# A window-attention and phase-mixing kernel: one transposition of batch 1 moved from a DMA to TensorE, inside a rewritten list of steps

## The chip, the cores and the metric

The kernel runs on one core of a Trainium2 chip. The metric is the device time of one launch in microseconds (us). The kernel before takes 169.82 us, the median of three runs (169.81, 169.82 and 170.51).

## What is computed

The reference is an attention layer followed by a mixing layer, for 4 batches (B), 8 heads (H), 768 tokens (S) and 64 numbers per head (D).

```python
scores = scale * np.matmul(q, k.transpose(0, 1, 3, 2)) + bias
keep = is_global | is_local            # 8 global keys, and the last 96 positions
a = softmax(np.where(keep, scores, -1e9))
x = np.matmul(a, v)  -> (B, S, H*D) = (4, 768, 512)
theta = x @ w_theta
zr, zi = x * np.cos(theta), x * np.sin(theta)
y = einsum('ts,bsd->btd', w_tok_r, zr) + einsum('ts,bsd->btd', w_tok_i, zi)
u = x + y
out = u + np.maximum(u @ w_ch, 0.0)
```

The bias is a slope of each head times the distance of key and query. The kernel computes in bf16 with sums in f32.

## The kernel before, in words

**Tiles.** Tokens are cut into six tiles of 128, heads are taken in four pairs (so a pair is 128 columns), and the 512 model columns are four chunks of 128, one for each pair. A query tile sees its own key tile, the tile before it and the 8 global keys; therefore the keys of a "tile before" are kept in a second copy (kG, values vG) whose first 8 rows are overwritten with the global ones.

**Steps.** Every piece of work is a small function (lines 198 to 565) that issues its instructions at once. A step is named by its function and its arguments: `m.1.2.0` is function `m_`, batch 1, token tile 2, part 0. For one batch the steps are:

- `lq`, `lv`: loads of q, k and v, issued by GpSimd (POOL) with a cast to bf16. Batch 3's q and k come in another layout (line 86). `lw`, `lt`, `lc` load the weights.
- `pc` (line 306, VectorE): regroups q or k of a pair so that `q` (line 294, TensorE, six 128x128 transpositions) can turn it; `qe` (line 299, VectorE or ScalarE by its letter v or a) copies the result from PSUM to qT or kT. For batch 3 `pd` (line 312) does all of this as one DMA transpose issued by SyncE (SP).
- `kg` (lines 322, 323): the copy kG.
- `s` (line 362, TensorE): scores of two token tiles; `e` (line 374, ScalarE): the exponential; `x` (lines 383, 386, VectorE): times a table of the bias; `v` (line 421, TensorE): times the values; `n` (lines 432, 434, VectorE): division by the sums, which gives a pair of x in x_sb.
- x has to be turned for the product with w_theta. Either `xd` (line 443) turns a pair as one DMA transpose, issued by SP, or `xt` (line 451, six 128x128 transpositions on TensorE into PSUM) and `xe` (line 456, the copy to xT on VectorE or ScalarE) do.
- `th` (line 477, TensorE): theta of two token tiles. Parts 0, 2 and 6 need pairs 0 to 2 of xT, part 3 needs pair 3. `sn` (lines 487, 489, ScalarE): cosine and sine; `z` (line 498, VectorE): times x.
- `m` (line 511, TensorE): a third of the 24 products of one output tile, four matmuls of 512 columns; `u` (line 519, VectorE): plus x. u is turned by `ud` (line 529, a DMA transpose from SP) or by `ut` (line 535) and `ue` (line 539). `c` (line 550, TensorE): times w_ch; `r` (line 558, VectorE): the final sum; `st` (line 564): the store, from SP, or from ScalarE's queue if its part is 1.

Steps that belong to no batch: `warm` (matmuls on zeros), `dist`, `diag`, `swap`, `bt` (tables of the bias), `sb` (the bias of batch 0's scores, laid into PSUM on TensorE), `w`/`we` (weights turned), `cast`, `mv` (ones beside v), `sin` (an activation on one column, which brings the sine table in), `gt` (a copy by which POOL waits for `z`).

**Order.** The whole order is written out by hand: `order` (line 572) is a list of 660 words, each a step, and every engine and queue works through its own part of the list in that order; nothing overtakes on an engine. Semaphores only hold an instruction until its inputs are there and its buffer is free. A step that waits therefore holds back what stands behind it on the same engine, and that goes for SP's queue of DMA transposes and stores too. The digits after the list (line 638) say which of the eight PSUM banks each step that writes PSUM takes.

**Buffers that matter here.** PSUM has eight banks for everything; xT has one buffer; the output tile `o` has four, so a fifth `r` waits for the store of the first; qkn (the regrouped pair) has two, uT five, e three.

In batch 1 the pairs 0 and 1 of x go by `xd`, the pairs 2 and 3 by `xt` and `xe`. In batch 2 the pairs 0 to 2 go by `xd`, pair 3 by `xt`; in batch 3 all go by `xd`.

Of the kernel before, what the change touches and what calls it, by code (L numbers as in the profile page):

```python
# [16 lines left out]
def kernel(  # L17
# [105 lines left out]
    dist = const.tile([T, 6, T], BF)  # L123
# [20 lines left out]
    diag = const.tile([T, H, T], BF)  # L144
# [422 lines left out]
    def do(op, *a):  # L567
        ops[op](*a)
# [1 line left out]


    order = """
        warm.1.3 diag.2 warm.6.0 dist diag.0 bt.6 diag.1 sb.0.1 cast.1.1.a cast.0.0.v warm.3.1 bt.0
        cast.0.1.a diag.3 cast.1.0.v bt.4 q.0.1.0 q.0.0.0 qe.0.1.0.v.2 q.0.0.1 qe.0.0.0.a.0
        qe.0.0.1.a.0 qe.0.0.0.a.1 q.0.1.1 kg.0.0.0.1.v qe.0.0.1.v.1 lw.0 sb.0.0 qe.0.1.1.a.2 swap
        s.0.0.0 kg.0.0.1.4.a sb.0.2 kg.0.1.0.4.v q.0.2.0 lt.0.2 e.0.0.0 q.0.2.1 qe.0.2.0.v.2 lt.2.4
        s.0.0.1 s.0.0.2 e.0.0.1 sb.1.0 qe.0.2.1.v.2 s.0.1.0 warm.1.2 e.0.1.0 sb.1.1 kg.0.2.0.4.v
        sb.1.2 vg.0.0.4 e.0.0.2 s.0.1.1 lw.2 s.0.1.2 sb.2.0 e.0.1.2 v.0.0.0.0.6 v.0.0.1.0.6 e.0.1.1
        s.0.2.0 n.0.0.1.0.6 lq.1.0.8 q.0.3.0 e.0.2.0 q.0.3.1 n.0.0.0.0.6 sb.2.1 qe.0.3.1.a.2
        qe.0.3.0.v.2 s.0.2.1 v.0.1.0.0.6 e.0.2.1 xt.0.0.0.6 sb.3.1 xe.0.0.0.6.v sb.3.0 kg.0.3.0.4.v  # L580
        sb.2.2 mv.1 s.0.2.2 s.0.3.1 n.0.1.0.0.6 e.0.2.2 s.0.3.0 v.0.1.1.0.6 vg.0.4.4 e.0.3.0 sb.3.2
        n.0.1.1.0.6 v.0.2.1.0.6 e.0.3.1 lw.4 v.0.3.2.0.2 n.0.2.1.0.6 s.0.3.2 v.0.2.0.0.6 e.0.3.2
        w.1.0 n.0.3.2.0.2 v.0.3.2.2.4 we.1.0.a w.0.0 n.0.3.2.2.4 xt.0.1.0.6 xt.0.3.0.2 n.0.2.0.0.6
        w.1.1 xe.0.1.0.6.a v.0.3.2.4.6 w.0.1 n.0.3.2.4.6 xe.0.3.0.2.a lc xt.0.2.0.6 bt.1 xt.0.3.2.4
        xt.0.3.4.6 xe.0.3.2.4.v bt.2 xe.0.2.0.6.v th.0.0.4 lv.1.0.8 we.0.1.v we.0.0.v th.0.0.5
        th.0.0.3 th.0.1.2 sn.0.0.0 lq.2.0.8 sn.0.0.1 w.2.0 z.0.0.0 th.0.1.3 xe.0.3.4.6.v w.2.1
        sn.0.1.0 z.0.0.1 th.0.2.2 mv.2 sn.0.1.1 we.1.1.v m.0.1.0 we.2.0.v sin.0 z.0.1.1 th.0.2.3
        m.0.0.0 z.0.1.0 sn.0.2.0 pc.1.1.0 w.3.1 lv.2.0.8 w.3.0 sn.0.2.1 z.0.2.0 q.1.1.0 m.0.0.1
        z.0.2.1 m.0.1.1 we.2.1.v m.0.0.2 pc.1.0.0 bt.3 we.3.1.v bt.7 m.0.1.2 pc.1.0.1 qe.1.1.0.a.2
        pc.1.1.1 we.3.0.v q.1.0.1 q.1.0.0 u.0.0 qe.1.0.1.a.2 q.1.1.1 m.0.2.0 pc.1.3.0 qe.1.0.0.a.2  # L590
        u.0.1 w.4.0 pc.1.2.0 ut.0.0 kg.1.0.0.4.v we.4.0.a m.0.2.2 qe.1.1.1.v.2 ue.0.0.a s.1.0.1
        pc.1.2.1 s.1.0.0 s.1.0.2 kg.1.1.0.4.v e.1.0.0 m.0.2.1 pc.1.3.1 lq.3.0.4 e.1.0.2 q.1.3.1
        m.0.3.0 qe.1.3.1.v.2 e.1.0.1 q.1.2.1 x.1.0.0 ut.0.1 c.0.0.2 ue.0.1.a qe.1.2.1.v.2 q.1.3.0
        x.1.0.2 c.0.1.2 qe.1.3.0.a.2 r.0.0.2 q.1.2.0 bt.5 x.1.0.1 s.1.1.1 qe.1.2.0.a.2 s.1.1.0 u.0.2
        m.0.3.2 r.0.1.2 e.1.1.0 m.0.3.1 kg.1.2.0.4.v e.1.1.1 x.1.1.0 w.4.1 u.0.3 s.1.2.0 s.1.1.2
        s.1.2.1 we.4.1.v e.1.1.2 m.0.4.0 vg.1.0.8 e.1.2.0 ut.0.2 m.0.4.1 ue.0.2.a x.1.1.1
        v.1.0.2.0.6 e.1.2.1 x.1.1.2 w.5.0 n.1.0.2.0.6 kg.1.3.0.4.a w.5.1 ut.0.3 v.1.1.2.0.6 we.5.0.a
        x.1.2.1 xd.1.0 s.1.3.0 ue.0.3.a n.1.1.2.0.6 m.0.4.2 we.5.1.a st.0.1.2 m.0.5.0 e.1.3.0
        x.1.2.0 xd.1.1 pc.2.0.0 s.1.2.2 u.0.4 s.1.3.1 e.1.2.2 s.1.3.2 st.0.0.2 m.0.5.2 pc.2.0.1
        e.1.3.2 x.1.2.2 q.2.0.0 pc.2.1.0 e.1.3.1 c.0.3.2 x.1.3.2 x.1.3.0 qe.2.0.0.a.2 v.1.2.2.0.6  # L600
        x.1.3.1 q.2.0.1 n.1.2.2.0.6 c.0.2.2 v.1.3.2.0.6 pc.2.3.0 pc.2.1.1 xt.1.2.0.6 n.1.3.2.0.6
        q.2.1.0 m.0.5.1 qe.2.1.0.a.2 xe.1.2.0.6.v q.2.1.1 qe.2.0.1.a.2 r.0.3.2 xt.1.3.0.6 th.1.0.0
        u.0.5 kg.2.0.0.4.a th.1.1.0 r.0.2.2 xe.1.3.0.6.a th.1.0.6 qe.2.1.1.v.2 ut.0.4 th.1.0.3
        pc.2.2.0 mv.3 th.1.1.6 kg.2.1.0.4.v sn.1.0.0 th.1.2.0 pc.2.2.1 ue.0.4.v sn.1.0.1 th.1.1.3
        z.1.0.0 ut.0.5 q.2.2.1 sn.1.1.0 th.1.2.6 z.1.0.1 m.1.0.0 vg.2.0.8 pd.3.1.0 sin.1 sn.1.1.1
        th.1.2.3 m.1.1.0 z.1.1.0 st.0.2.2 sn.1.2.0 z.1.1.1 c.0.4.2 gt.1.2 sn.1.2.1 z.1.2.0 lq.3.4.4
        m.1.1.1 r.0.4.2 qe.2.2.1.a.2 m.1.0.1 z.1.2.1 ue.0.5.v s.2.0.2 s.2.0.0 s.2.0.1 m.1.0.2
        e.2.0.0 m.1.1.2 e.2.0.1 u.1.0 c.0.5.2 ud.1.0 e.2.0.2 u.1.1 s.2.1.1 r.0.5.2 s.2.1.0 ud.1.1
        s.2.1.2 e.2.1.0 x.2.0.1 m.1.2.0 lv.3.0.8 pc.2.3.1 pd.3.0.0 x.2.0.0 e.2.1.1 m.1.3.0 x.2.0.2
        q.2.2.0 x.2.1.1 pd.3.2.1 q.2.3.1 qe.2.2.0.a.2 m.1.2.1 qe.2.3.1.v.2 kg.2.2.0.4.a q.2.3.0  # L610
        m.1.2.2 e.2.1.2 qe.2.3.0.v.2 s.2.2.0 u.1.2 s.2.2.2 s.2.2.1 e.2.2.0 x.2.1.2 m.1.3.2 ud.1.2
        e.2.2.1 x.2.2.0 v.2.0.2.0.6 pd.3.1.1 kg.2.3.0.4.v m.1.5.0 e.2.2.2 n.2.0.2.0.6 m.1.3.1
        st.0.3.2 x.2.1.0 xd.2.0 s.2.3.2 x.2.2.1 s.2.3.0 s.2.3.1 e.2.3.0 m.1.5.1 kg.3.2.0.4.v
        st.0.5.2 u.1.3 e.2.3.2 m.1.5.2 x.2.2.2 e.2.3.1 x.2.3.2 c.1.1.2 x.2.3.0 kg.3.1.0.4.a
        v.2.2.2.0.6 x.2.3.1 v.2.1.2.0.6 n.2.2.2.0.6 m.1.4.0 n.2.1.2.0.6 xd.2.2 v.2.3.2.0.6 c.1.0.2
        n.2.3.2.0.6 xd.2.1 m.1.4.1 r.1.1.2 m.1.4.2 pd.3.0.1 r.1.0.2 xt.2.3.0.6 u.1.4 th.2.0.0
        st.0.4.2 xe.2.3.0.6.a u.1.5 pd.3.3.1 th.2.1.0 kg.3.0.0.4.a th.2.0.6 st.1.0.2 th.2.1.6 ud.1.4
        kg.3.3.0.4.v th.2.0.3 th.2.2.0 sn.2.0.0 ud.1.5 th.2.1.3 th.2.2.6 sn.2.0.1 ud.1.3 c.1.2.2
        sin.2 sn.2.1.0 z.2.0.1 c.1.5.2 pd.3.2.0 z.2.0.0 sin.3 sn.2.1.1 th.2.2.3 r.1.2.2 m.2.0.0
        st.1.1.2 z.2.1.0 sn.2.2.0 pd.3.3.0 z.2.1.1 m.2.1.0 r.1.5.2 sn.2.2.1 c.1.3.2 z.2.2.0 m.2.0.1  # L620
        r.1.3.2 z.2.2.1 s.3.0.0 s.3.1.0 e.3.0.0 vg.3.0.8 s.3.0.2 m.2.1.2 e.3.1.0 m.2.1.1 x.3.0.0
        e.3.0.2 m.2.0.2 u.2.1 s.3.2.0 u.2.0 s.3.0.1 e.3.2.0 s.3.2.1 x.3.1.0 m.2.2.0 ud.2.0 e.3.2.1
        c.1.4.2 e.3.0.1 m.2.2.2 r.1.4.2 x.3.0.1 s.3.1.2 s.3.3.0 e.3.1.2 s.3.1.1 x.3.2.1 m.2.3.0
        x.3.0.2 e.3.1.1 x.3.2.0 v.3.0.2.0.6 x.3.1.1 m.2.2.1 e.3.3.0 n.3.0.2.0.6 m.2.3.2 u.2.2 xd.3.0
        s.3.2.2 s.3.3.2 s.3.3.1 e.3.2.2 m.2.3.1 e.3.3.2 ud.2.2 x.3.2.2 m.2.4.0 x.3.1.2 e.3.3.1
        x.3.3.2 st.1.2.2 v.3.1.2.0.6 x.3.3.0 st.1.5.2 v.3.2.2.0.6 u.2.3 m.2.4.2 x.3.3.1 n.3.2.2.0.6
        v.3.3.2.0.6 c.2.0.2 n.3.1.2.0.6 xd.3.2 m.2.5.0 n.3.3.2.0.6 xd.3.1 c.2.2.2 m.2.4.1 ud.2.1
        m.2.5.1 u.2.4 xd.3.3 th.3.0.0 th.3.1.0 st.1.4.2 th.3.0.6 ud.2.3 m.2.5.2 ud.2.4 th.3.0.3
        u.2.5 th.3.1.6 sn.3.0.0 th.3.2.0 st.1.3.2 sn.3.0.1 th.3.1.3 z.3.0.0 th.3.2.6 sn.3.1.0
# [20 lines left out]
_INS = ['q', 'k', 'v', 'n_global', 'n_local', 'moe_w_theta', 'moe_w_tok_r', 'moe_w_tok_i', 'moe_w_ch']  # L650
_OUTS = [((4, 768, 512), 'float32')]
# [30 lines left out]
```

## Time and profile before

| what | us |
|---|---|
| median of three runs | 169.82 |
| the profiled execution's own time | 170.19 |
| its span, from its first to its last instruction | 168.1 |
| TensorE (PE) busy | 154.2 |
| VectorE (DVE) busy | 124.8 |
| ScalarE (ACT) busy | 106.6 |
| GpSimd (POOL) busy | 38.5 |

The profile is one execution. "Busy" of PE overstates its work: matmuls are pipelined, and a matmul's row is longer than the distance to the next one. Idle time in a row is given in brackets with what ended it. DMA rows of SP and POOL show only the issuing; when a transfer lands is told by "to landing" and by the DMA pieces in the chain of waits. Times in the views are us from the start of the span.

### The profile page before, as it was taken

The page shows a single profiled execution, that of the slowest core. Times are in us where ns is not written, and L with a number is a line of the kernel's source. Part 1 is how long each engine was busy: PE and PEld are TensorE (multiplying, and loading weights), DVE is VectorE, ACT ScalarE, POOL GpSimd, SP SyncE. Part 2 cuts the span into 40 slices and gives each one's busy share as a digit, 9 for nine tenths or more (in the row PEclk, how much of TensorE's full clock was granted, in tenths as well). Part 3 has the DMA queues.
Part 4 walks back from the last instruction along what each step waited for, and adds up shares of the span by engine and source line. Part 5 has one row for each costly group of instructions (what it writes and reads, how often), then busy time and mean ns, then how long its engine had stood idle before and what let it go on. Part 6 is the DMA issues. An engine that isn't in the chain of part 4 may idle for free.

```text
span 168.1 us, 3796 instructions
## 1 busy us (share of the span) xinstructions
PE 154.2 (92%) x1547; PEld 86.2 (51%) x1569; DVE 124.8 (74%) x257; ACT 106.6 (63%) x142; POOL 38.5 (23%) x46
## 2 busy tenths in 40 slices
PE   7899999999999996999987798899999999999990
PEld 2456685555657573545553543345557444444450
DVE  7697986978999998695994991588789438543571
ACT  3899899898789937898866115988871349100010
POOL 8975348050352102079400000000000000000000
PEclk9999999999999999999999999999999999999999
DMA  5999999999999999989999998560125674344456
GB/s 150 199 171 177 209 209 203 204 208 188 149 199 193 148 191 149 78 137 121 154 118 146 205 108 207 113 156 4 31 47 158 127 172 174 100 44 125 125 206 231
DMA packets 72704, 25.34 MB, mean 151 GB/s; under 512 B 60784, under 2 KB 69744, under 8 KB 72688
## 3 DMA queue, kind: packets, MB, share of 16 engines
q0 software_dynamic: 45696, 12.45, 82.0%
q1 hardware_dynamic: 26576, 12.13, 34.8%
q10 hardware_dynamic: 416, 0.52, 0.9%
q8 instruction: 12, 0.20, 0.5%
q14 instruction: 4, 0.03, 0.1%
HBM read 25.69 MB, written 6.29 MB: 190 GB/s over the span
## 4 chain that ended last, share of the span: by engine, by line
PE 59%; DMA 18%; DVE 15%; issue 2%; SPq 2%; ACT 1%; POOL 0%; DVEq 0%; POOLq 0%
PE bank L511 27%; PE bank L477 9%; PE bank L550 9%; DMA kT<-qk 8%; DMA xT<-x_sb 6%; PE bank L362 4%; PE bank L421 4%; DMA qk<-in_q_dram 3%; DVE e L383 2%; DVE x_sb L434 2%; DVE kT L299 2%; PE bank L265 2%; SPq L312 1%; DMA uT<-u 1%; DVE kG L322 1%
## 5 line engine op out<-in xcount | busy, mean ns | idle before, releaser
L511 PE MATMUL bank<-zri,w_tokT 128*128 128x512 bf16 x273 | 66.8, 379 | 1.4 <-issue 1.0
L374 ACT ACTIVATE e<-bank 128x1024 bf16<-128x1024 f32 (+1 forms) x48 | 42.9, 955 | 8.9 <-PE bank L362 8.3
L511 PEld LDWEIGHTS <-w_tokT 128*128 128x128 bf16 x288 | 26.5, 98 | 29.5 <-DVE w_tokT L269 0.2
L550 PE MATMUL bank<-w_ch_bf,uT 128*128 128x512 bf16 (+1 forms) x98 | 24.1, 370 | 2.4 <-DVE u L519 1.6
L477 PE MATMUL bank<-w_theta_bf,xT 128*128 128x512 bf16 x92 | 22.8, 379 | 2.9 <-DMA xT<-x_sb 2.7
L519 DVE TENSOR_TENSOR u<-x_sb,bank 128x512 bf16<-128x512 bf16 x24 | 16.2, 684 | 11.2 <-PE bank L511 11.0
L558 DVE SCALAR_TENSOR_TENSOR o<-bank,u 128x512 f32<-128x512 f32 (+1 forms) x25 | 16.2, 666 | 7.9 <-PE bank L550 7.5
L498 DVE TENSOR_TENSOR zri<-x_sb,cs 128x1024 bf16<-128x1024 bf16 (+1 forms) x30 | 16.6, 580 | 6.1 <-ACT cs L489 4.0
L434 DVE TENSOR_TENSOR x_sb<-bank,rec 128x768 bf16<-128x768 f32 (+2 forms) x21 | 16.1, 767 | 0.7
L550 PEld LDWEIGHTS <-uT 128*128 128x128 bf16 x100 | 9.3, 98 | 12.3 <-issue 1.8
L477 PEld LDWEIGHTS <-xT 128*128 128x128 bf16 x96 | 8.8, 97 | 13.0 <-DMA xT<-x_sb 3.9
L539 ACT COPY uT<-bank 128x512 bf16<-128x512 bf16 x5 | 2.9, 589 | 19.1 <-PE bank L535 19.1
L383 DVE TENSOR_TENSOR e<-e,etab 128x1024 bf16<-128x1024 bf16 (+1 forms) x24 | 14.1, 618 | 0.9 <-ACT e L374 0.9
L421 PEld LDWEIGHTS <-e 128*128 128x128 bf16 x352 | 12.6, 97 | 3.3 <-issue 1.0
L362 PE MATMUL bank<-qT,kT 64*128 64x128 bf16 x224 | 12.9, 218 | 0.4 <-DVE qT L299 0.3
L421 PE MATMUL bank<-vn,e 128*128 128x65 bf16 x224 | 13.2, 193 | 0.1
L489 ACT ACTIVATE cs<-bank,halfpi 128x1024 bf16<-128x1024 f32 x8 | 8.9, 1116 | 6.2 <-PE bank L477 6.2
L362 PEld LDWEIGHTS <-kT 64*128 64x128 bf16 x224 | 8.6, 94 | 6.3 <-issue 5.4
L92 POOL DMA_DIRECT2D vn<-in_v_dram x5 | 9.6, 1922 | 8.1 <-DVE qkn L306 6.9
L362 PE MATMUL bank<-qT,kG 64*128 64x128 bf16 x128 | 10.7, 216 | 0.0
L421 PE MATMUL bank<-vG,e 128*128 128x65 bf16 x128 | 10.4, 193 | 0.1
L86 POOL DMA_DIRECT2D qk<-in_q_dram x8 | 6.9, 864 | 12.4 <-issue 4.7
(76 smaller groups left out, 199.1 us busy)
## 6 DMA issues: line engine op xcount, KB each, us to landing
out_dram<-o SPq DMA_DIRECT2D x23, 256.0 KB, 2.4
vn<-in_v_dram POOLq DMA_DIRECT2D x3, 768.0 KB, 23.1
qk<-in_q_dram POOLq DMA_DIRECT2D x2, 768.0 KB, 20.3
qk<-in_k_dram POOLq DMA_DIRECT2D x2, 768.0 KB, 22.3
w_nat<-in_moe_w_tok_r_dram POOLq DMA_DIRECT2D x3, 384.0 KB, 12.3
w_nat<-in_moe_w_tok_i_dram POOLq DMA_DIRECT2D x3, 384.0 KB, 13.5
vn<-in_v_dram POOLq DMA_DIRECT2D x2, 384.0 KB, 9.8
qk<-in_q_dram POOLq DMA_DIRECT2D x8, 96.0 KB, 9.5
```

The source lines that it names most:

```text
L92: nc.gpsimd.dma_start(out=vn[:, h0:h0 + n, :, 0:D].rearrange("p h t d -> p (h t) d"), in_=v[b, h0:h0 + n].rearrange("h (t p) d -> p (h t) ...
L362: nc.tensor.matmul(pb[:, hh, o:o + T], lhsT=lhsT, rhs=qT[R, (own, nxt)[part]], start=bool(b), stop=bool(b) or (jt == NT - 1 or (j == 1 and ...
L374: nc.scalar.activation(e_c, ps_of["s", b, p, c][:, :, 0:blocks(c) * T], AF.Exp, scale=scale)
L383: nc.vector.tensor_mul(e_c, e_c, tab[:, :, s0:s0 + n].rearrange("p a s n -> p a (s n)"))
L421: nc.tensor.matmul(po4[:, head - h0, it - i0], lhsT=l_, rhs=r_, start=(i_ == 0), stop=(i_ == len(mms) - 1))
L434: nc.vector.tensor_mul(xv, po4[:, :, :, 0:D], rec.to_broadcast([T, m_, nt, D]))
L477: nc.tensor.matmul(ps_of["th", b, c][j_], lhsT=xT_sb[b][:, dc, (2 * c + j_) * T:(2 * c + j_ + 1) * T], rhs=w_theta_bf[:, dc, :], start=(dc ...
L498: nc.vector.tensor_mul(zri[b][:, i_, tt, :].rearrange("p j (g d) -> p j g d", g=NP), x_sb[b][:, :, tt, :].rearrange("p g j d -> p j g d"), ...
L511: nc.tensor.matmul(ps_of["m", b, tt], lhsT=w_tokT[wi][:, st, tt * T:(tt + 1) * T], rhs=zri[b][:, wi, st, :], start=(mixed[b, tt] == 0), st ...
L519: nc.vector.tensor_add(u_sb[b, tt].rearrange("p (g d) -> p g d", g=NP), x_sb[b][:, :, tt, :], ps_of["m", b, tt].rearrange("p (g d) -> p g ...
L550: nc.tensor.matmul(ps, lhsT=uTs[b, tt][:, dc, :], rhs=w_ch_bf[:, dc, own], start=(dc == 0), stop=(dc == NC - 1))
L558: nc.vector.scalar_tensor_tensor(o_sbs[b, tt][:, own], in0=ps_of["c", b, tt, part], scalar=0.0, in1=u_sb[b, tt][:, own], op0=ALU.max, op1= ...
```

## The change

Pair 1 of batch 1's x is turned by TensorE and copied out of PSUM by VectorE: `xd.1.1` leaves the list, `xt.1.1.0.6` and `xe.1.1.0.6.v` come in. The list then has 661 words. All other steps remain, but the list is a new one from its first word to its last, with new bank digits (191 for 190). Twenty-nine copies changed engine, among them (before to after) `qe.2.2.0` and `qe.2.2.1` from ScalarE to VectorE, `kg.2.3` and `kg.1.2` from VectorE to ScalarE, `kg.2.2` and `kg.3.1` from ScalarE to VectorE, `xe.1.3` and `xe.2.3` from ScalarE to VectorE, `ue.0.4` and `ue.0.5` from VectorE to ScalarE.

The core of the diff, around the end of batch 1's attention and in batch 2 (all other lines of the list differ too; no function differs):

```diff
     order = """
...
-        v.1.0.2.0.6 e.1.2.1 x.1.1.2 w.5.0 n.1.0.2.0.6 kg.1.3.0.4.a w.5.1 ut.0.3 v.1.1.2.0.6 we.5.0.a
-        x.1.2.1 xd.1.0 s.1.3.0 ue.0.3.a n.1.1.2.0.6 m.0.4.2 we.5.1.a st.0.1.2 m.0.5.0 e.1.3.0
-        x.1.2.0 xd.1.1 pc.2.0.0 s.1.2.2 u.0.4 s.1.3.1 e.1.2.2 s.1.3.2 st.0.0.2 m.0.5.2 pc.2.0.1
...
+        n.1.1.2.0.6 xd.1.0 s.1.3.0 s.1.2.1 u.0.4 e.1.3.0 st.0.1.2 ut.0.3 xt.1.1.0.6 ue.0.3.v m.0.5.0
+        pc.2.0.0 e.1.2.1 xe.1.1.0.6.v s.1.3.1 pc.2.0.1 s.1.2.2 pc.2.1.0 s.1.3.2 e.1.3.1 x.1.2.1
...
+        n.1.3.2.0.6 th.1.0.0 sin.1 ue.0.4.a xt.1.3.0.6 kg.2.0.0.4.a th.1.0.6 xe.1.3.0.6.v th.1.1.0
...
-        v.2.2.2.0.6 x.2.3.1 v.2.1.2.0.6 n.2.2.2.0.6 m.1.4.0 n.2.1.2.0.6 xd.2.2 v.2.3.2.0.6 c.1.0.2
-        n.2.3.2.0.6 xd.2.1 m.1.4.1 r.1.1.2 m.1.4.2 pd.3.0.1 r.1.0.2 xt.2.3.0.6 u.1.4 th.2.0.0
...
+        st.0.4.2 pd.3.3.0 x.2.3.2 v.2.1.2.0.6 sin.3 c.1.2.2 n.2.1.2.0.6 xd.2.2 c.1.1.2 r.1.0.2
+        xd.2.1 m.1.5.1 x.2.3.1 v.2.3.2.0.6 pd.3.2.1 m.1.5.2 n.2.3.2.0.6 ud.1.3 m.1.4.2 r.1.1.2
+        m.1.4.1 r.1.2.2 pd.3.1.1 kg.3.2.0.4.v th.2.0.0 u.1.5 pd.3.0.0 xt.2.3.0.6 th.2.0.6
```

SP's queue, the transposes and stores alone, from batch 1's x to the last transpose of batch 3's q and k:

```
before: xd.1.0 st.0.1 xd.1.1 st.0.0 pd.3.1.0 st.0.2 ud.1.0 ud.1.1 pd.3.0.0 pd.3.2.1 ud.1.2 pd.3.1.1
        st.0.3 xd.2.0 st.0.5 xd.2.2 xd.2.1 pd.3.0.1 st.0.4 pd.3.3.1 st.1.0 ud.1.4 ud.1.5 ud.1.3
        pd.3.2.0 st.1.1 pd.3.3.0
after:  xd.1.0 st.0.1 st.0.3 st.0.0 pd.3.0.1 ud.1.0 ud.1.2 ud.1.1 st.0.2 xd.2.0 st.0.5 st.0.4
        pd.3.3.0 xd.2.2 xd.2.1 pd.3.2.1 ud.1.3 pd.3.1.1 pd.3.0.0 st.1.1 ud.1.5 pd.3.3.1 pd.3.1.0
        st.1.0 st.1.3 pd.3.2.0 ud.1.4
```

POOL's loads keep their order; only the place of the waiting copy `gt.1.2`, of `lq.3.4.4` and of `lv.3.0.8` among the other engines' steps is new.

## The prediction

> **What bounds the kernel.** I read the page's busy line and the forty slices first, then the chain of waits, then TensorE's (PE's) timeline, and last the DMA issues with their landings.
>
> ```profile
> span 168.1 us, 3796 instructions
> ...
> PE 154.2 (92%) x1547; PEld 86.2 (51%) x1569; DVE 124.8 (74%) x257; ACT 106.6 (63%) x142; POOL 38.5 (23%) x46
> ...
> PE   7899999999999996999987798899999999999990
> ```
>
> PE is busy all the way but for dents at slices 15 and 21 to 25, so PE's own work plus PE's waits make the time. PE's work, at the pace that the chain shows (8 matmuls of 512 columns in 1.73 us, 22 of scores in 0.72, 22 of values in 0.67, six transpositions in 0.35), is: 476 x 0.2155 + 8 halves 0.9 = 103.5; scores 11.4; values 10.7; 238 transpositions of 128x128 13.4; batch 0's q and k 3.4; bias 4.6; warm 2.4; together 149.4. Of 168.05 there remain 18.65: 4.2 spent before PE is in steady work (at 8.4 us), 4.3 behind its last matmul, 4.5 in switches of 0.05 to 0.16, and 5.6 in six gaps. These are the gaps, in PE's timeline (start, duration, group, idle time before it and its releaser):
>
> ```profile
> 65.30 1.67 PE L477 MATMUL bank<-w_theta_bf,xT 128*128 128x512 bf16 x7 [1.57 <-DMA xT<-x_sb]
> ...
> 81.97 0.51 PE L294 MATMUL bank<-ident,qkn 128*128 128x128 bf16 x6 [0.35 <-DVE qkn L306]
> ...
> 85.36 0.21 PE L362 MATMUL bank<-qT,kT 64*128 64x128 bf16 x1 [0.27 <-DVE qT L299]
> ...
> 93.22 1.02 PE L550 MATMUL bank<-w_ch_bf,uT 128*128 128x512 bf16 x4 [1.56 <-DVE u L519]
> ...
> 101.59 2.76 PE L477 MATMUL bank<-w_theta_bf,xT 128*128 128x512 bf16 x11 [1.13 <-DMA xT<-x_sb]
> ...
> 107.90 1.04 PE L550 MATMUL bank<-w_ch_bf,uT 128*128 128x512 bf16 x4 [0.74 <-DMA uT<-u]
> ```
>
> The first is the transposition that the change takes away. The chain says what lies behind this and the others (start, duration, piece):
>
> ```profile
> 55.59 9.44 DMA xT<-x_sb
> ...
> 81.91 10.14 DMA kT<-qk
> ...
> 105.41 2.44 DMA uT<-u
> ```
>
> A DMA transpose lands 2.4 to 2.8 us after its issue when nothing else moves, and 5 to 10 us after it while POOL's loads run: the V load issued at 79.44 lands 15.7 us later, and all transposes issued from 77.8 to 89.7 take 5.1 to 10.1. The 1.56 at 93.22 is of that kind too: DVE stood at kG (line 322) until the 10.14 us transpose had landed, and u behind it.
>
> **The parts.** The whole list is new, so I counted through the new one: each step stands at the sum of PE's work ahead of it, and its time is that sum plus what PE has lost so far (in the old list 5.9 us at the first theta, 6.6 at batch 1's, 14.3 at the end; this reproduces its rows within 0.2).
>
> *Transposition of pair 1.* Added on PE and DVE are a set like those of these two groups (by shape: count, busy time and mean ns, idle before):
>
> ```profile
> L451 PE MATMUL bank<-ident,x_sb 128*128 128x128 bf16 x42 | 3.5, 219 | 0.0
> ...
> L456 DVE COPY xT<-bank 128x768 bf16<-128x768 bf16 x3 | 1.7, 552 | 0.1
> ```
>
> Six at 0.35 us a set: +0.35, all on the path. The copy of 0.55 on DVE lies beside PE: the new list has 54.0 us of DVE work ahead of th.1.0.0, the old one 53.8, because other copies left DVE. If that cover failed, it would cost its 0.55. Removed: an SP issue (1.35) and the landing at 65.03. What is late next? xe.1.1 stands 49.3 deep in PE's work, about 56; pair 0's DMA stays, issued near 52.5, and took 7.4 (two landings have the median 8.4, one is 9.44), so it is in by 60; pair 2's copy ends near 62.5. th.1.0.0 stands 56.9 deep, at 63.2. All three are in, so the 1.57 goes. Pair 3's transposition now has n.1.3 (1.13 on DVE) directly ahead of it: +0.3 (0 to 0.6).
>
> [...]
>
> *81.97 and 85.36.* The first gap comes from one copy on DVE:
>
> ```profile
> 80.03 1.88 DVE L306 COPY qkn<-qk 128x768 bf16<-128x768 bf16 x1
> ```
>
> The other 15 of its line mostly take 0.35; this one met POOL issuing the V load (79.44, for 2.28). The new list has pc.2.3.0, pc.2.3.1, kg.2.1 and kg.2.2 before that issue, but beside batch 3's q/k issues (0.8 each). A vG copy met such issues at 49.66 and lost 0.2 at most, so DVE, with a wait of 1.79 for PE at 75 to 77 as its slack, carries it. Both gaps go: -0.62. In their place qe.2.2.0, now on DVE after x.2.0.1, ends near 82.1 where s.2.2.0 could start at 81.9: +0.3 (0 to 1.0).
>
> [...]
>
> *93.22.* In the old list four transposes went out at 77.8 to 81.9 into the loads. In the new one pd.3.2.1 stands behind ud.1.2, ud.1.1, xd.2.0, xd.2.2 and xd.2.1. In exchange ud.1.2 and ud.1.1 go out when u.1.2 is done, near 84.8 and 86.1, and c.1.2.2 and c.1.1.2 want them at 91 and 92. The V load goes out near 77.5, two earlier, with fewer transposes beside it; an undisturbed one took 6.2 (the weights ahead of it landed at 41.55, it at 47.77), so it may be in by 88 to 91. With the 8.5 that ud.1.2 took before they would come at 93.3; with the 5.1 of ud.1.0 at 90. Cost 0 to 2.3; I take 0.5, nearer to 5.1 because the load is nearly through. -1.56 +0.5.
>
> *101.59.* xd.2.1 waits for n.2.1 (about 92.2), goes out near 93.1 and lands at 96 to 97; th.2.0.0 stands 89.4 deep, at 97. Cost 0 to 4 (if it took 8.3); I take 0.4. -1.13 +0.4.
>
> *107.90.* ud.1.5 goes out near 100 and lands at 102.5, c.1.5.2 comes at 103.3: -0.74. But kg.3.2 and kg.3.1 stand on DVE just behind transposes issued at 94.3 and 97, with u.1.5, xe.2.3, u.1.4 and z.2.0.0 behind them: +0.2 (0 to 2.5).
>
> *Batch 3 to the end.* xd.3.3 waits on SP behind st.2.1, whose r.2.1 needs the store of r.1.2; it lands within 0.5 of th.3.0.3's turn: +0.5 (0 to 1.2). The last six steps end alike.
>
> *Start.* ACT makes five bias tables before the casts instead of two more at 24.0; the first exponential can start near 9.65 (before 10.09), but vG (lands 13.06 and 18.1) and xe.0.2 on DVE take most of it back: -0.2 (-0.7 to +0.5).
>
> **Sum.** -5.62 (all six gaps) +0.35 +0.3 +0.3 +0.5 +0.4 +0.2 +0.5 -0.2 = -3.3. Against the profiled execution (168.05 span, 170.19 with what lies around it) that is 166.9; it lay 0.4 above the median of the runs, so against 169.82 it is **166.5**.
>
> **Rivals.**
>
> *Only the change's own wait goes.* The other four gaps are late landings that a list with as many transposes may meet again elsewhere. For it: with loads on the way, seven of the old list's transposes took 5.1 to 10.1, and the new list issues as many. Against: it issues fewer of them between 77 and 85. -1.57 +0.35 +0.3 +0.5 -0.2 = -0.6: 169.2, within 0.5%. Chance 0.14.
>
> *SP's queue of batch 3's transposes runs late (slower).* Seven of the eight `pd` now stand behind ud.1.2 and xd.2.x. If the V load is still on its way at 93, xd.2.1 takes 8.3 and holds th.2.0.0 until 101.4 (+4.4), pd.3.2.1 takes 10.1 and holds DVE at kG until 104.5, and xe.2.3 behind it ends 1.1 later, while th.2.0.3 wants it at 103.6 (+2.0); with c.1.2.2 at its 2.3 the sum is -3.3 -1.1 +2.3 +4.4 +2.0 = +4.3, less where they overlap (1.5): 172.6. It decides from a landing of the V load later than about 93. For it: the old one landed at 95.09. Against: it starts earlier. With smaller delays of this kind, 0.24.
>
> *The change doesn't do what it says.* If xd.1.0, left alone on the queue, landed as late as 65, th.1.0.0 would still wait: +1.6, 168.1. Its landing at 61 in the old trace speaks against it. 0.07, on the faster side.
>
> The forecast has 0.55; its own range is 163.9 (every new wait nothing, start -0.7) to 168.3. About 0.5% is what a measurement of this kernel can tell from no change. Faster by more 0.62, within 0.14, slower by more 0.24. For 8 in 10 the range goes up to 171.5, which leaves out the upper part of the slow case.
>
> **What would show it.** Right: no theta matmul waits for xT in batch 1; the copy at line 306 takes 0.35 throughout; the V load of batch 3 lands before 92; PE waits under 2.5 us between 60 and 110. Wrong: a kG or xT landing 7 to 10 us after issue near 95, DVE standing at line 322 for microseconds, or PE reaching the first theta later than 24.6.

## The result, and the profile after

The kernel after takes **167.81 us** (median of 4 runs, 167.07 to 168.26) against 169.86 for the kernel before beside it (169.81 to 170.51): ratio 0.9867, 95% interval 0.9831 to 0.9904. Twelve more runs later gave 168.25, ratio 0.9910 (0.9875 to 0.9944). Executions more than 1.5% above the fastest of their kernel are left out of the ratios, here and below, but not out of the medians. So it is 0.9 to 1.3% faster, 1.5 to 2.3 us by the two ratios; forecast were 3.3. Its profiled execution took 168.26 with a span of 166.0 (before: 170.19 and 168.1).

From the profile's page of the kernel after, busy time of the engines and TensorE's share of 40 slices:

```profile
span 166.0 us, 3834 instructions
...
PE 156.5 (94%) x1575; PEld 86.5 (52%) x1575; DVE 125.6 (76%) x262; ACT 104.7 (63%) x138; POOL 38.6 (23%) x46
...
PE   7899899999999999999999979989999899999990
```

Counted from 0, the old row has its dents at slices 15, 20 to 22, 24 and 25. They are gone; a 7 and two 8 are there, near 98, 110 and 131 us. TensorE's timeline of the kernel after names them (start, duration, group, idle time before it and its releaser):

```profile
19.99 0.19 PE L421 MATMUL bank<-vG,e 128*128 128x65 bf16 x1 [0.62 <-DVE vG L398]
...
98.86 0.60 PE L477 MATMUL bank<-w_theta_bf,xT 128*128 128x512 bf16 x2 [0.91 <-DMA xT<-x_sb]
...
101.37 2.98 PE L477 MATMUL bank<-w_theta_bf,xT 128*128 128x512 bf16 x13 [0.28 <-DVE xT L456]
...
110.04 0.23 PE L362 MATMUL bank<-qT,kT 64*128 64x128 bf16 x2 [0.61 <-DVE o L558]
...
132.95 0.81 PE L477 MATMUL bank<-w_theta_bf,xT 128*128 128x512 bf16 x3 [0.65 <-DVE u L519]
```

Not one of the six old gaps is among them, except that theta of batch 2 again waits for its last transpose (98.86). The other four are new. What lies behind three of them stands in the chain of waits from 95.4 to 110 us (start, duration, piece; pieces of under 0.1 us are left out):

```profile
95.42 0.68 SPq L443
96.20 3.53 DMA kT<-qk
99.76 0.30 DVE kG L322
100.09 0.18 DVE kG L323
100.26 0.59 DVE u L519
100.85 0.48 DVE xT L456
101.37 0.62 PE bank L477 x2
102.02 2.04 ACT cs L489 x2
104.24 1.23 SPq L312
105.52 1.28 SPq L312
106.85 2.35 DMA out_dram<-o
109.30 0.70 DVE o L558
```

Read it from below: the sum at 109.30 waited for a store's buffer, the store for two transposes ahead of it on SP, each 1.23 to 1.28 us of issuing. Higher up, xT's copy at 100.85 stood behind u, u behind kG, and kG behind the transpose to kT, which SP issued only at 96.20. From 85.8 to 110.6 SP issues 15 transposes and 6 stores with no pause of over 0.2 us.

For the comparisons below I use TensorE's *loss*: the start of a step less all of TensorE's work ahead of it, as in the prediction. A stretch's loss is what it adds. Each column is one profiled execution (e5 and e12 are second profiles of the kernels after and before); "forecast" is the column before with the prediction's terms added stretch by stretch, without the 0.35 us of added work. Two profiles of one kernel (before and e12, after and e5) agree within 0.4 us in every stretch behind the first theta:

| stretch (us) | before | e12 | forecast | after | e5 | e1 | e3 | e4 | e9 | e11 |
|---|---|---|---|---|---|---|---|---|---|---|
| to the first theta (26) | 5.72 | 5.72 | 5.5 | 6.80 | 5.88 | 5.56 | 5.82 | 6.50 | 6.48 | 6.26 |
| to theta of batch 1 (64) | 0.90 | 0.90 | 0.9 | 0.59 | 0.60 | 1.33 | 0.60 | 0.59 | 0.59 | 0.60 |
| its first matmuls (67) | 1.37 | 1.55 | 0.1 | 0.00 | 0.00 | -0.16 | 0.00 | 0.00 | 0.00 | 0.00 |
| to s.2.3.0 (87) | 1.58 | 1.60 | 1.3 | 0.80 | 0.80 | 1.77 | 0.81 | 0.81 | 0.80 | 0.80 |
| to theta of batch 2 (97) | 1.96 | 1.55 | 0.9 | -0.19 | -0.20 | 0.37 | -0.19 | -0.19 | -0.19 | 0.39 |
| to th.2.0.3 (101) | 1.15 | 1.11 | 0.6 | 1.74 | 1.82 | 1.35 | 1.87 | 0.93 | 0.70 | 0.37 |
| to s.3.0.0 (110) | 1.23 | 1.00 | 0.5 | 0.78 | 0.80 | 0.83 | 0.10 | 1.83 | 1.68 | 0.22 |
| to the end | 0.38 | 0.38 | 0.9 | 1.56 | 1.23 | 0.37 | 0.51 | 1.20 | 0.51 | 0.64 |
| sum | 14.29 | 13.81 | 10.7 | 12.08 | 10.93 | 11.42 | 9.52 | 11.67 | 10.57 | 9.28 |

### The profile page after: what moved, and what is told of

The parts are those of the page before. It is cut to its first block, busy times and chain, and to the rows that moved or that the text cites. A ratio compares the mean times of both kernels' runs of the same rounds, so it can differ in the third digit from the quotient of the medians.

```text
span 166.0 us, 3834 instructions
## 1 busy us (share of the span) xinstructions
PE 156.5 (94%) x1575; PEld 86.5 (52%) x1575; DVE 125.6 (76%) x262; ACT 104.7 (63%) x138; POOL 38.6 (23%) x46
## 4 chain that ended last, share of the span: by engine, by line
PE 66%; DMA 14%; DVE 7%; POOL 4%; SPq 4%; issue 2%; ACT 2%; DVEq 0%; POOLq 0%; ACTq 0%
PE bank L511 31%; PE bank L477 9%; PE bank L550 8%; DMA vn<-in_v_dram 7%; PE bank L362 5%; DMA out_dram<-o 4%; PE bank L421 4%; PE bank L294 3%; POOL qk L77 3%; PE bank L265 2%; DMA kT<-qk 2%; DVE o L558 2%; SPq L312 2%; DVE x_sb L434 1%; ACT cs L489 1%
## 5 line engine op out<-in xcount | busy, mean ns | idle before, releaser
L511 PE MATMUL bank<-zri,w_tokT 128*128 128x512 bf16 x288 | 68.7, 379 | 0.0
L383 DVE TENSOR_TENSOR e<-e,etab 128x768 bf16<-128x768 bf16 (+1 forms) x24 | 14.6, 618 | 2.9 <-ACT e L374 2.7
L539 ACT COPY uT<-bank 128x512 bf16<-128x512 bf16 x4 | 2.3, 585 | 17.9 <-PE bank L535 17.9
L421 PE MATMUL bank<-vG,e 128*128 128x65 bf16 x128 | 10.2, 193 | 0.7 <-DVE vG L398 0.6
```

The costliest lines, as they stand in the source:

```text
L383: nc.vector.tensor_mul(e_c, e_c, tab[:, :, s0:s0 + n].rearrange("p a s n -> p a (s n)"))
L421: nc.tensor.matmul(po4[:, head - h0, it - i0], lhsT=l_, rhs=r_, start=(i_ == 0), stop=(i_ == len(mms) - 1))
L511: nc.tensor.matmul(ps_of["m", b, tt], lhsT=w_tokT[wi][:, st, tt * T:(tt + 1) * T], rhs=zri[b][:, wi, st, :], start=(mixed[b, tt] == 0), st ...
```

## The experiments

| kernel | median us (runs) | ratio to before, 95% |
|---|---|---|
| e1 swap alone, old list | 167.77 (10) | 0.9907, 0.9873 to 0.9940 |
| e2 new list without the swap | 168.47 (12) | 0.9925, 0.9885 to 0.9965 |
| e3 two stores earlier | 166.00 (6) | 0.9827, 0.9766 to 0.9888 |
| e4 xd.2.2, xd.2.1 earlier | 168.07 (12) | 0.9931, 0.9900 to 0.9962 |
| e5 after again | 168.25 (12) | 0.9910, 0.9875 to 0.9944 |
| e6 V load late | 175.38 (6) | 1.0326, 1.0283 to 1.0369 |
| e7 V load early, old list | 168.38 (12) | 0.9928, 0.9899 to 0.9957 |
| e8 vG copy later | 168.26 (12) | 0.9927, 0.9900 to 0.9954 |
| e9 e3, e4, e8 and more | 166.68 (6) | 0.9849, 0.9810 to 0.9888 |
| e10 old start | 168.60 (12) | 0.9932, 0.9902 to 0.9962 |
| e11 six stores from ScalarE | 165.95 (6) | 0.9782, 0.9746 to 0.9819 |
| e12 before again | 170.25 (10) | 1.0007, 0.9979 to 1.0034 |

Single runs of one kernel differ by up to 2% (before: 167.81 to 171.12 in 27 runs), so differences under 0.5 us are read from the profiles' stretches, not from the medians.

**Theory** after the result: the swap ends one wait, the new list four of the other five, and what is missing from the forecast went into SP's full queue near 100 us and into the start. **Rivals**: the swap alone does it all; the new list does it all; the remaining waits come from the loads.

### The two parts apart: e1 and e2

e1, on the list before:

```diff
- x.1.2.0 xd.1.1 pc.2.0.0
+ x.1.2.0 pc.2.0.0
- q.2.0.0 pc.2.1.0 e.1.3.1
+ q.2.0.0 xt.1.1.0.6 pc.2.1.0 xe.1.1.0.6.v e.1.3.1
```

> The kernel before, its list kept, with only the transposition of pair 1 of batch 1 changed: xd.1.1 is taken out, xt.1.1 stands behind q.2.0.0 (about 57.6 us) and its copy behind pc.2.1.0 on VectorE. Theory: TensorE's own wait of 1.57 us for xT at 65.3 goes, six more transpositions cost 0.35, and the other five gaps between 82 and 108 us stay, as they come from where transposes and loads meet later. That is 1.2 less: 168.7 us (168.2 to 169.2). Rival A: what is won at 65 is given back in the gaps at 82 to 108, since the loads of batch 3 decide there: 169.4 to 170. Rival B: the later gaps hang on this wait too and shrink with it: under 168.

Measured: 1.6 us less than before by the ratio (1.0 to 2.2), and by the spans of the profiles 2.0 to 2.5 (165.6 against 167.6 and 168.1). Rival B holds: besides the 1.57, the gap at 93 is gone, in a list that has not changed there. That gap is read from one profile of e1; the ten times, 166.92 to 168.35, fit it, as the theory without it has 168.2 to 169.2. Other gaps of the old list stay: 0.53 at 81.23, 0.27 at 84.62, 1.34 at theta of batch 2 and 0.33 at 105.37. VectorE's timeline of e1, and below it that of e12, the kernel before:

```profile
89.74 0.29 DVE L322 COPY kG<-kT 128x512 bf16<-128x512 bf16 x1 [0.64 <-DMA kT<-qk]
```

```profile
91.86 0.29 DVE L322 COPY kG<-kT 128x512 bf16<-128x512 bf16 x1 [1.82 <-DMA kT<-qk]
```

TensorE came to this point 0.7 to 0.9 us earlier than before, but kG had its input 2.1 earlier: the transpose to kT went out at 80.97 in place of 82.04 and took 8.75 in place of 9.79.

e2, on the list after:

```diff
- st.0.1.2 ut.0.3 xt.1.1.0.6 ue.0.3.v
+ st.0.1.2 xd.1.1 ut.0.3 ue.0.3.v
- e.1.2.1 xe.1.1.0.6.v s.1.3.1
+ e.1.2.1 s.1.3.1
```

> The kernel after, its new list kept, with pair 1 of batch 1 back on the DMA: xt.1.1 and xe.1.1 are taken out, xd.1.1 goes out behind st.0.1.2 (about 56 us). Theory: the list brings most of the gain, and the named change its own wait: the transpose lands at 64.5 to 66, th.1.0.0 or th.1.0.6 stands for it 0.6 to 1.6 us near 64, 0.35 of transpositions is saved: 168.1 to 169.0 us, likeliest 168.5. Rival: in the new order the second transpose lands in time as well (pair 0's now lands at 61.9), so that the change of engine alone only costs: 167.5 us. A second rival: the wait is longer than before, 2 us or more: over 169.4.

Measured: 168.47, as expected, 1.3 us less than before by the ratio (0.6 to 2.0). In its profile, of an execution of 169.37, the transpose lands at 66.06 and theta waits for it:

```profile
66.11 0.60 PE L477 MATMUL bank<-w_theta_bf,xT 128*128 128x512 bf16 x2 [1.48 <-DMA xT<-x_sb]
```

The gap at 93 is gone here too. So the parts alone give 1.6 and 1.3 us, and both together 1.5 to 2.3, not 2.9. By time neither part can be told from the whole change (167.77 and 168.47 against 167.81 and 168.25). The intervals are wide; that the gains do not add rests on the profiles, where each part alone removes the gap at 93, which can be won only once. What the swap is worth inside the new list stays open: by e2's profile about the 1.48 less 0.35, by the medians (168.47 against 168.25) next to nothing.

### Is the gap at 93 chance? e12

The kernel before, unchanged.

> The kernel before, unchanged, for a second profile. With the swap alone (e1) TensorE's wait of 1.56 us at 93.2 was gone too, though that kernel changes nothing near there: kT landed 8.75 us after its issue in place of 10.14. Theory A: the wait belongs to the old list with its two DMA transposes of x; a second profile shows kT landing 9.5 us or more after its issue near 82 and TensorE waiting 1 to 2 us for u near 93. Theory B: the landings beside the V load scatter by 1 to 2 us from one execution to the next, TensorE's margin there is about nothing, and the second profile shows a wait under 0.7 us. Its times: 169.9 us, ratio 1.00.

Theory A: kT took 9.79 us and TensorE waited for u again:

```profile
93.00 1.02 PE L550 MATMUL bank<-w_ch_bf,uT 128*128 128x512 bf16 x4 [1.15 <-DVE u L519]
```

The gap belongs to the kernel before, so e1's loss of it is real. Why the transpose then takes 1.0 to 1.4 less is not settled.

### SP's queue: e3, e4, e9, e11

e3, on the list after (SP's steps alone are shown, here and in the next two):

```diff
- ud.1.5 pd.3.3.1 pd.3.1.0 st.1.0.2
+ ud.1.5 st.1.0.2 pd.3.3.1 pd.3.1.0
...
- ud.2.1 xd.3.0 ud.2.2 xd.3.1 ud.2.0 st.1.2.2
+ ud.2.1 st.1.2.2 xd.3.0 ud.2.2 xd.3.1 ud.2.0
```

> The kernel after, with two stores issued earlier on SP's queue and nothing else changed: st.1.0.2 directly behind ud.1.5 (ahead of two transposes of batch 3), st.1.2.2 directly behind ud.2.1 (some 9 us earlier). Theory: the stores hold back the final sums r.1.5 (VectorE waits 1.44 us at 109.3) and r.2.1 (1.36 us at 130.5) by the four output buffers, and through them TensorE waits 0.61 us at 110.0 and 0.65 at 132.95. All four waits go: 1.2 less, 166.6 us (166.3 to 167.0). Rival: TensorE's scores at 110 and theta at 133 are held by other things just behind (the exponential, u of batch 2), and it wins under 0.4: 167.4 to 167.8.

Measured: 166.0. The gaps at 110 and 133 are gone, and behind the first theta TensorE loses 3.70 us where it lost 5.28 and 5.05 in the two profiles of after.

e4, on the list after:

```diff
- xd.2.0 st.0.5.2 st.0.4.2 pd.3.3.0 xd.2.2 xd.2.1 pd.3.2.1
+ xd.2.0 xd.2.2 st.0.4.2 xd.2.1 pd.3.2.1 st.0.5.2 pd.3.3.0
```

> The kernel after, with another order on SP's queue near 91 us: xd.2.2 right behind xd.2.0, then st.0.4.2, xd.2.1, pd.3.2.1, st.0.5.2, pd.3.3.0 (it was xd.2.0, st.0.5.2, st.0.4.2, pd.3.3.0, xd.2.2, xd.2.1, pd.3.2.1). Theory: SP issues one thing after the other, 1.3 us a transpose and 0.6 a store, so xd.2.1 goes out at 94.8 though its input is there at 93.2. Now it goes out near 93.3 and lands by 97.2; the transpose to kT goes out 1.6 us earlier, and with it kG, u.1.5 and xe.2.3 on VectorE. TensorE's waits of 0.91 us at 98.9 and 0.28 at 101.4 go: 1.2 less, 166.6 us (166.3 to 167.1). Rival: VectorE still stands at kG until the transpose to kT lands, and theta's last chunk behind xe.2.3 waits instead: under 0.4 less, 167.4 to 167.8.

Measured: 168.07, nothing won: the rival. The 0.91 goes, but the wait at xe.2.3 grows to 0.56, and c.1.5.2 now waits for uT, because ud.1.5 still goes out at 102.86:

```profile
105.34 1.04 PE L550 MATMUL bank<-w_ch_bf,uT 128*128 128x512 bf16 x4 [0.79 <-DMA uT<-u]
```

One stretch gives 0.8 to 0.9, the next takes 1.0.

e9: e3, e4 and e8 (below) together, `ud.1.5` behind `u.1.5`, `pd.3.1.1` behind it, and on VectorE `kg.3.1` behind `vg.3`.

```diff
- ud.1.3 pd.3.1.1 pd.3.0.0 st.1.1.2 ud.1.5 pd.3.3.1 pd.3.1.0 st.1.0.2
+ ud.1.3 ud.1.5 pd.3.1.1 pd.3.0.0 st.1.1.2 st.1.0.2 pd.3.3.1 pd.3.1.0
```

> The kernel after with the edits of e3_stores, e4_xd_first and e8_v_copy_later together, and two more: ud.1.5 goes out directly behind u.1.5, ahead of pd.3.1.1, pd.3.0.0 and the stores of batch 1, and kg.3.1 stands behind vg.3 on VectorE. Theory: between 86 and 112 us SP issues without a pause, so a transpose is late by what stands ahead of it; e4 alone only shifted the wait to uT (0.79 at 105.3) because ud.1.5 kept its place. In order of need, the waits at 98.9, 101.4, 105.3, 110.0 and 133 all go: e3's 166.0 less 1.3 at theta of batch 2 and 0.3 at the start: 164.4 us (163.8 to 165.4). Rival: SP is simply full there, and whatever is moved back is missed next (the transposes of batch 3, wanted by the scores at 109 to 113): 165.6 to 166.4.

Measured: 166.68, not better than e3 alone. TensorE's timeline of e9:

```profile
109.36 0.34 PE L362 MATMUL bank<-qT,kT 64*128 64x128 bf16 x6 [1.61 <-DMA qT<-qk]
```

What was moved back is missed next: a transpose of batch 3, landed at 109.22. Of these moves only e3's paid: nothing came to wait for what its two stores pushed back.

e11 takes work off it. On the list after, `st` gets a part 3, a whole row from ScalarE's queue, and six stores use it: three behind `sin.3`, three behind `r.1.2`. SP's steps, and two copies on VectorE:

```diff
-        own = cols(part)
-        (nc.scalar if part == 1 else nc.sync).dma_start(
+        own = cols(2 if part == 3 else part)
+        (nc.scalar if part in (1, 3) else nc.sync).dma_start(
...
- st.0.2.2 xd.2.0 st.0.5.2 st.0.4.2 pd.3.3.0 xd.2.2 xd.2.1 pd.3.2.1 ud.1.3 pd.3.1.1 pd.3.0.0 st.1.1.2 ud.1.5
+ xd.2.0 xd.2.2 pd.3.3.0 xd.2.1 pd.3.2.1 ud.1.3 ud.1.5 pd.3.1.1 pd.3.0.0
- pd.3.3.1 pd.3.1.0 st.1.0.2 st.1.3.2
+ pd.3.3.1 pd.3.1.0 st.1.3.2
...
- kg.3.2.0.4.v u.1.5 xe.2.3.0.6.v kg.3.1.0.4.v
+ u.1.5 xe.2.3.0.6.v kg.3.2.0.4.v
- vg.3.0.8
+ vg.3.0.8 kg.3.1.0.4.v
```

> The kernel after, with six stores (of rows 0.2, 0.5, 0.4, 1.0, 1.1, 1.2) issued from ScalarE's queue in place of SP's, between 90 and 98 us where ScalarE has nothing to do for 10 us; on SP xd.2.2 is put ahead of pd.3.3.0 and ud.1.5 ahead of pd.3.1.1; on VectorE kg.3.2 is put behind xe.2.3 and kg.3.1 behind vg.3. Theory: SP's time is what is short between 86 and 112 us (23 issues back to back). Six stores are 3.4 us of it. With them gone, TensorE's waits at 98.9 (0.9 to 1.1), 101.4 (0.28), 110.0 (0.62) and 133 (0.3 to 0.65) go, and nothing takes their place: 2.2 less than the kernel after, 165.6 us (165.0 to 166.2), and between the first theta and the end TensorE loses 2.9 us where it lost 5.1. Rival: as in e4 and e9, the transposes' own turns on SP (17 of 1.3 us) fill it, and the next transpose is missed: no better than the two stores of e3, 166.0 to 166.8.

Measured: 165.95, the fastest of all with e3: 2.2% less than before. Behind the first theta TensorE loses 3.02 us (expected 2.9), from 97 us to the end 1.23 where e3 loses 2.48. Its waits (engine, line, cause: us in all, times, longest):

```profile
PE bank L550 <- DMA uT<-u: 0.4, 1, 0.4
...
PE bank L477 <- DMA xT<-x_sb: 0.2, 1, 0.2
```

The 0.4 is new: three stores from ScalarE went out at 87.4 to 88.3 beside the V load, and a transpose issued at 86.56 took 6.01. By time e11 and e3 can't be told apart. By the stretches the loss before th.2.0.3, 1.87 us in e3, is 0.37 here, and it does not come back behind it as in e4 and e9: SP's turns were short there. But e11 also reorders transposes and copies, and like e3 it sends st.1.0 and st.1.2 early; what the six stores alone are worth is not shown.

### The loads: e7 and e6

e7, on the list before:

```diff
- pc.2.2.0 mv.3 th.1.1.6
+ pc.2.2.0 mv.3 lv.3.0.8 th.1.1.6
...
- m.1.2.0 lv.3.0.8 pc.2.3.1
+ m.1.2.0 pc.2.3.1
```

> The kernel before, with only batch 3's V load moved ahead on GpSimd's queue: lv.3 directly behind mv.3, so that it goes out near 67 us, before the second half of batch 3's q and k loads and not behind it at 79.4. Theory: what makes the DMA transposes between 80 and 90 us land 6 to 10 us after their issue is the V load beside them (15.65 us itself). Without it there they land in 2.5 to 5 us, VectorE does not stand at kG, and TensorE's waits of 1.56 at 93.2 and most of the 1.13 at 101.6 and 0.74 at 107.9 go: 2.5 less (1.5 to 3.4), 167.2 us. Rival: the delay comes from several transposes in a row on SP's queue and from the q and k loads; then the landings stay at 5 to 10 us and the time at 169.3 to 169.9.

Measured: 1.2 us less by the ratio (0.7 to 1.7), about half of what was expected. The gap at 93 shrinks to 0.27 and those of 82 and 85 go, but the transposes of 78 to 89 still take 4.7 to 8.4: now the q and k loads, pushed back by the V load, land beside them until 88.6. So it need not be V's load: in this run those of q and k lay beside them. None of the new waits near 100, 110 and 133 us in the kernel after falls beside a load: its last one, V, lands at 89.72. So the rival that they come from the loads does not hold there.

e6, on the list after: GpSimd waits for n.2.0 before it issues the V load.

```diff
+    def gx_(b, p):
+        nc.gpsimd.tensor_copy(out=gate, in_=x_sb[b][0:1, p, 0, 0:1])
...
- s.2.1.1 lv.3.0.8 r.0.5.2
+ s.2.1.1 r.0.5.2
- n.2.0.2.0.6 ud.1.2
+ n.2.0.2.0.6 gx.2.0 lv.3.0.8 ud.1.2
```

> The kernel after, with batch 3's V load held back by about 9 us: a copy of one element of x behind n.2.0 on GpSimd, and lv.3 behind it, so that it goes out near 87 us and not at 78.3 (it landed at 89.7). This makes the case of the slower rival: a V load that is still on its way at 93. By that rival the transposes for theta of batch 2 and for kG (xd.2.1, pd.3.2.1) then take 7 to 10 us in place of 3.5 to 4, theta waits 3 to 4 us at 98, VectorE stands at kG: 170 to 172.5 us. Against it: by then the q and k loads are in, and the V load by itself slows a transpose by 2 us at most: 168.0 to 169.2.

Measured: 175.38, 3.3% slower than before and worse than the rival's own price. TensorE's timeline (the lines lie 5 lower in this kernel, so L482 is theta), and SP's:

```profile
105.43 1.04 PE L482 MATMUL bank<-w_theta_bf,xT 128*128 128x512 bf16 x2 [7.52 <-DMA xT<-x_sb]
```

```profile
94.53 7.08 SPq L448 DMA_TRANSPOSE xT<-x_sb  x2
101.71 2.08 SPq L317 DMA_TRANSPOSE kT<-qk  x1
```

The V load went out at 87.52 and landed at 104.57. Transposes issued at 91.75, 94.53 and 97.06 took 12.19, 10.24 and 8.33 us, and SP itself stood 2.4 to 4.5 us at each. Theta waits 6.6 longer than in after. There ud.1.2, issued at 85.79 beside the V load, took 4.41 us against 2.4 alone, so 2 more, as in the expectation's "2 us at most"; here the three took 5.6 to 9.4 more than the 2.7 to 2.8 that they take alone.

### The start: e5, e8, e10

e5 is the kernel after, unchanged.

> The kernel after, unchanged, for more of its times and a second profile beside the next kernels. Theory on its start: TensorE waits 0.62 us at 20 us for vG, since the second half of batch 0's V load landed at 19.02; in other profiles of the same list it landed between 18.05 and 18.80, and TensorE reached the first theta between 24.6 and 25.4. Expected: median 167.8 us (167.4 to 168.2), the first theta at 24.6 plus what V lands later than 18.1. Rival: the later start belongs to the list whatever V does: first theta at 25.3 or later with an early V.

Measured: a median of 168.25, just above the expected range. Its V load landed at 18.11, the first theta (here: its first weight load) came at 24.69. e2, e3, e4, e6 and e11 share this start. With after and e5, the seven first thetas come 6.57 to 6.59 us behind V's landing (18.05 to 19.02), one for one. In four profiles of the old start (before, e1, e7, e12) V lands at 18.09 to 18.43 and the first theta comes at 24.37 to 24.54, no later for a later V; a landing later than 18.43 was not seen with it.

e8, on the list after:

```diff
- vg.0.4.4 sb.3.0 s.0.3.0 n.0.1.1.0.6 v.0.2.0.0.6 e.0.3.0 v.0.1.0.0.6 xe.0.0.0.6.v
+ sb.3.0 s.0.3.0 n.0.1.1.0.6 xe.0.0.0.6.v vg.0.4.4 e.0.3.0 v.0.1.0.0.6
- s.0.3.1 n.0.2.0.0.6 lw.4 sb.3.2 e.0.3.1 s.0.3.2 n.0.1.0.0.6
+ s.0.3.1 lw.4 sb.3.2 v.0.2.0.0.6 n.0.1.0.0.6 n.0.2.0.0.6 e.0.3.1 s.0.3.2
```

> The kernel after, with batch 0's second vG copy (vg.0.4.4) put behind n.0.1.1 and xe.0.0 on VectorE, and the values of pair 2 (v.0.2.0) behind those of pair 1, the scores s.0.3.1 and the bias sb.3.2 on TensorE, as it was roughly in the list before; n.0.1.0 and n.0.2.0 follow. Theory: the new list asks for vG about 1.2 us earlier than the old one, and a V load that lands after 18.1 holds TensorE directly. With the copy later a landing up to 19 costs nothing, TensorE reaches the first theta near 24.7: 0.6 less than the kernel after, 167.2 us (166.8 to 167.6). Rival: the first theta is set by something else that lands late too (the weights), and nothing changes: 167.6 to 168.0.

Measured: 168.26, nothing won. V landed at 19.06, the first theta came 6.59 behind it as ever. My edit put n.0.1.0 behind the vG copy too, and the weight's transposition w.0.0 waited 0.74 us for that bank: the same wait at another door, so the size of the start's cost was not tried by this.

e10, on the list after, has the old list's first 122 steps with their banks in place of its own; behind them:

```diff
- th.0.0.4 lv.1.0.8 we.1.0.v sin.0 xe.0.3.2.4.a we.1.1.v th.0.0.5 xe.0.3.4.6.v
+ th.0.0.4 lv.1.0.8 we.0.1.v we.0.0.v sin.0 th.0.0.5
```

> The kernel after with the first 122 steps (up to the first theta) in the order of the list before, with their banks; the steps that the two lists have on different sides of that point are moved along (weight copies we.0.0, we.0.1, we.1.1, the copy xe.0.3.4, the table bt.5, mv.2), and th.0.0.4 and th.0.1.2 take other banks. Theory: in six profiles of the new list the first theta comes at 24.6 us plus all that batch 0's second V load lands after 18.1; in three of the old list it comes at 24.4 to 24.5 with landings of 18.1 to 18.4. So the new start costs what V is late, 0.5 us on average: first theta at 24.3 to 24.7 even with a landing of 18.7 to 19.1, and 167.5 us (167.1 to 167.8). Rival: the old start is no better with such a late V, or the loss comes back behind the first theta: first theta at 25.2 or later with a landing of 18.7 or more, 167.8 to 168.4.

Measured: 168.60, not faster. V landed early in its profile (17.97), so the profile doesn't test the landing, and TensorE lost 0.29 and 0.46 us behind the first theta, waiting for ScalarE's cosines. That the new start rides on V's landing is shown by its seven landings; that the old one, put back, would save the time is not.

## Why the prediction was right or wrong

**Right: what bounds it, and that five of the six gaps go.** 4.6 to 4.7 of 5.6 us are gone; the sixth, at theta of batch 2, hardly moved (0.91 in after and 1.01 in e5, of 1.13). Pair 1's set of six transpositions took 0.37 us (55.58, its first weight load, to 55.95; the row of one is 219 ns), its copy 0.54 beside other work, and pair 0's DMA landed at 61.88, 2 us later than forecast and still 2.4 before its turn. The copy of 1.88 us at line 306 did not come back: all 16 took 0.34 to 0.56. The V load landed at 89.72, within my 88 to 91.

**Wrong: whose gain it is.** The step "*Only the change's own wait goes* ... 169.2" held the other gaps for a matter of the list. e1 shows that the swap alone, in the old list, ends the gap at 93 as well, and brings 1.6 us. By the medians of e5 the whole change is worth about half of the forecast.

**Wrong sizes, term by term.**
- Start, "-0.2 (-0.7 to +0.5)": it measured +1.1 in the profile of after and +0.2 in e5. I noted V's landing of 18.1 and did not ask what a landing of 19 would do to a list that copies vG 1.2 us earlier. This is 0.92 of the 1.15 us between after (loss 12.08) and e5 (10.93); the forecast, made from an early V, was 10.7. My own sign of being wrong, TensorE reaching the first theta later than 24.6, came true: 25.66 in after.
- 93.22, "+0.5": it cost nothing; ud.1.2 and ud.1.1 landed at 90.20 and 90.64, before their turns at 91.7 and 92.4.
- 101.59, "+0.4", and "+0.2" for kG: 0.91 and 0.28. "goes out near 93.1" failed: its input was there at 93.22, but SP had st.0.5, st.0.4 and pd.3.3.0 to issue ahead of xd.2.2 and it, and got to it at 94.84. I added up landings, not SP's turns.
- "107.90 ... -0.74": uT's wait went, but the scores of batch 3 now wait 0.61 for r.1.5, which waits for a store behind two transposes. I had looked at the stores of batch 3 only.
- End, "+0.5": the gap is 0.65 in after and 0.31 in e5, right in place (r.2.1 behind the store of r.1.2). The stretch as a whole lost 1.2 and 0.9 more than in before, so the term was too small.

Against the forecast column, after is 2.0 us better in the stretches to 64, 67, 87 and 97, and 3.4 worse in the others. That the sum is off by no more than 1.4 is in part luck.

**The slower rival** was priced at 172.6 with a V load "still on its way at 93". In after it landed at 89.72 and the rival did not happen; e6 made it happen and it cost more than said: SP's own issuing stops too (2.4 to 4.5 us at a transpose), and behind the wait TensorE runs at a granted clock of 0.50 until about 110.6 (see the end), which adds 1.8 us to nineteen matmuls. The rival's margin in after is 3 us (89.72 against 93).

**What the change takes away** is a landing among loads. The transpose of 55.59 took 9.44 us, and st.0.0, a plain store that SP issued at 56.98 in the same profile, took 8.62. With nothing else moving a store took about 2.4 there and a transpose 2.4 to 2.8.

e6's 12.19, 10.24 and 8.33 us stand against 2.7 to 2.8 alone. SP's transfers land there in the order of their issue, at 96.00, 96.97, 97.83, 103.94, 104.76 and 105.39, so these times may hold a wait for the ones before. The one of 12.19 landed 6.1 us behind the one before it, about twice its time alone. How much of that is the V load's doing is not shown.

## What to carry to other kernels

A queue that issues without a pause (SP in after: 15 transposes and 6 stores from 85.8 to 110.6 us) is to be counted like an engine: add up its turns, here mostly 1.2 to 1.3 us a transpose and 0.4 to 0.6 a store, before forecasting when a transfer "goes out". A new order of it paid where what was pushed back was not missed (e3, 166.00 us), and only moved the wait where it was (e4, 168.07; 1.61 us at 109.36 in e9); taking work off it (e11, 165.95) was as fast as the best new order. Two changes that each ended the same wait did not add up (e1 1.6 us, e2 1.3, both 1.5 to 2.3), so try the small one alone first. When a list is rearranged, ask of every load's consumer how late the load may come (the start), for a landing seen once is not a constant: batch 0's V landed at 18.05 to 19.02 in seven profiles of one start.

## What the runs showed of the hardware

- A transpose held its issuer: in e6 SP stood 4.5 us at the one it issued at 97.06, while the two transposes before it were still on their way (they landed at 103.94 and 104.76). What let it go at 101.6 no row tells.
- The granted clock fell in e6 during theta's wait of 7.5 us: 1.00 until 100, 0.58 from 100 to 102, then 0.50 until 110 and 0.72 from 110 to 111, though TensorE was busy again from 105.43. By these shares it stood at one half from 100.3 to 110.6. The nineteen matmuls from 106.90 on took 5.9 us until the next step began at 112.81, where 0.2155 each makes 4.1. Full clock was back about 5 us after the restart at 105.43, and about 10.2 us after the fall; this is one case, and what sets these times is not shown.
